# Letting V run four blocks ahead at the start of the last pass, preparing the tail, and holding three stores back

## The chip, the cores and the metric

The kernel runs on one core of one Trainium2 chip. The time is device microseconds of one execution. A profile shows one execution, and single executions of these kernels differ by several microseconds, so times are judged from the timed runs and the profiles are read for where the time goes.

## The reference, cut to what matters

Two layers, each grouped-query attention of one token over a cache of 65,536 positions (32 query heads on 4 K/V heads, head size 128), and a feed-forward block with squared ReLU, then the gradient of everything. Both layers share K, V and the weights.

```python
def _A_ref(x, k_cache, v_cache, wq, wo):        # cut
    q = (x @ wq) ...
    p = softmax(q k^T * Dh**-0.5); o = p v
    return o @ wo
x = x + A(layernorm(x)); x = x + B(layernorm(x))   # twice, same weights
_out, _vjp = jax.vjp(_f, A_x, A_k_cache, A_v_cache, A_wq, A_wo, B_w1, B_b1, B_w2, B_b2)
return (_out, *_vjp(grad_out))
```

The gradients of K and V are as large as the caches: 128 MB of stores, nearly all in the last pass.

## The kernel before: what the change and the argument touch

The kernel makes four passes over K and V. The last one, `attn_bwd4`, walks 4 groups of 16 blocks (a block is 32 x 128 positions of V or K, 1 MB) in steps of 8 columns, 256 items in all. Per block it turns V (`vT`), forms dP and X (`vS`), makes dV (`dV8`), and with K adds to dq and makes dK (`k8`). Each result block is stored.

```python
pipeline(items, [(vT, 0), (vS, TLEAD), (dV8, DV_LAG), (k8, B4_LAG)], bg, end)

def outer16(name, out, key, xt, gg, j1):          # dV and dK, cut
    if j1 == 0:
        state[key] = Slot(name, True)             # a result takes a slot ...
    ...
        evac(stg[:, jj:jj + 8, :]..., pg[:, :], kind="f32")
    if j1 + 16 == J:
        nc.gpsimd.dma_start(out=out, in_=stg)
        state.pop(key).free(stored=True)          # ... and gives it back once stored
```

Loaded blocks and finished results share one arena of 20 slots of 1 MB. Eight of these hold E (what earlier passes left for both layers) when the last pass begins; two come free at the end of each group, so blocks and results have 12 slots in the first group and 18 in the last. Loads are issued by SP, stores by GpSimd (POOL in the profile). Which free slot a load of the last pass takes is this rule (`AHEAD` is 9 steps):

```python
if load and PS["pass4"]:
    early = [i for t, i in by_age if t <= NOW["step"] - AHEAD]
    i = early[-1] if early else by_age[0][1]
```

At the end, after the last K matmuls give dq, the gradient of wq for the last group is made from rows of dq and of the layer input by eight rank-2 products (`g_outer`), stored as two pieces of 1 MB.

## Time and profile before

| what | before |
|---|---|
| time, median of the first 3 runs | 2013.33 us (2010.8 to 2014.11) |
| profiled span | 2015.4 us |
| busy share PE / DVE / ACT | 80 / 58 / 52% |
| bytes moved, mean rate | 794.97 MB, 394 GB/s |
| last pass | from about 1205 us on |

How to read it: at the full rate of about 420 GB/s the transfers fill most of the span, so only stretches with a lower rate can be won. In the last pass these are the opening and the end. The lines are in the prediction.

### The profile page before, as it was taken

To read this page: it belongs to the slowest core of one execution; us is meant where nothing else is said; L and a number is where in the kernel's file an instruction comes from. 1 tells how busy PE (TensorE), PEld (TensorE's weight loads), DVE (VectorE), ACT (ScalarE), POOL (GpSimd) and SP (SyncE) were. 2 spreads that over 40 slices of the span, in tenths; PEclk is the share of its full clock that TensorE was granted. 3 is DMA by queue.
4 is the path that set the end of the run, shared out by engine and by line. 5 is a ranking of instruction groups with operands and counts; after the bars stand their busy time and mean duration, and the time that the engine had idled before them with its cause. 6 is when DMAs were issued, how large, how long until landed. Compare 5 with 4: busy or idle time off the path is not lost. (4 is left out here: it accounts for less than half of the span.)

```text
span 2015.4 us, 67001 instructions
## 1 busy us (share of the span) xinstructions
PE 1613.8 (80%) x30210; PEld 1315.4 (65%) x30210; DVE 1175.3 (58%) x2358; ACT 1043.6 (52%) x1613; POOL 144.4 (7%) x332
## 2 busy tenths in 40 slices
PE   6877787687887787868787888788778988698896
PEld 6877777677777686767777785455445555455554
DVE  5655455255555544535454476586658777577675
ACT  3444344253443353426354365586657677577675
POOL 0000000000000000000000001121111111121111
PEclk9999899699899997999888998799879889798888
DMA  9999999999999998999999986999999999999995
GB/s 389 420 419 420 419 422 399 391 406 419 420 417 419 420 404 316 371 420 420 418 413 417 394 305 254 363 404 424 421 405 404 408 419 399 358 405 424 416 377 236
DMA packets 110845, 794.97 MB, mean 394 GB/s; under 512 B 9424, under 2 KB 9438, under 8 KB 49374
## 3 DMA queue, kind: packets, MB, share of 16 engines
q1 hardware_dynamic: 86510, 624.99, 76.3%
q0 software_dynamic: 24048, 165.70, 19.9%
q8 instruction: 236, 3.87, 0.8%
q14 instruction: 51, 0.42, 0.1%
HBM read 624.96 MB, written 165.69 MB: 392 GB/s over the span
## 5 line engine op out<-in xcount | busy, mean ns | idle before, releaser
L153 DVE COPY kt<-ps_tr 128x1024 bf16<-128x1024 bf16 x724 | 497.7, 689 | 481.3 <-PE ps_tr L936 255.4
L150 ACT CAST arena<-ps_gg 128x1024 bf16<-128x1024 f32 x452 | 440.0, 1010 | 226.0 <-PE ps_gg L1303 169.7
L936 PE MATMUL ps_tr<-ident_b,arena 128*128 128x128 bf16 x3840 | 311.3, 226 | 55.7 <-DMA arena<-in_A_k_cache_dram 41.4
L936 PEld LDWEIGHTS <-arena 128*128 128x128 bf16 x3840 | 235.2, 101 | 62.3 <-DMA arena<-in_A_k_cache_dram 44.4
L153 DVE CAST arena<-ps_gg 128x1024 bf16<-128x1024 f32 (+1 forms) x191 | 228.9, 1199 | 77.3 <-PE ps_gg L1303 43.6
L150 ACT COPY kt<-ps_tr 128x1024 bf16<-128x1024 bf16 x164 | 172.3, 1055 | 185.9 <-PE ps_tr L1128 125.7
L1303 PE MATMUL ps_gg<-GG,xt 64*128 64x512 bf16 x1024 | 214.1, 417 | 46.3 <-DVE arena L153 26.1
L1038 PE MATMUL ps_acc<-arena 128*128 128x64 bf16 (+4 forms) x4096 | 204.7, 195 | 49.4 <-DMA arena<-in_A_v_cache_dram 28.9
L1249 PE MATMUL ps_tr<-ident_b,arena 128*128 128x128 bf16 x1824 | 178.2, 236 | 39.7 <-DMA arena<-in_A_v_cache_dram 38.8
L954 PE MATMUL ps_sc<-L_qpad,kt 128*128 128x64 bf16 (+7 forms) x3584 | 183.9, 194 | 19.6 <-issue 12.3
L1019 ACT ACTIVATE arena<-S_sb,L_negm 128x128 bf16<-128x128 f32 x256 | 165.7, 1003 | 58.2 <-DVE L_negm L1004 58.2
L1128 PE MATMUL ps_tr<-ident_b,arena 128*128 128x128 bf16 x1920 | 155.8, 227 | 46.5 <-DMA arena<-in_A_v_cache_dram 45.2
L1038 PEld LDWEIGHTS <-arena 128*128 128x128 bf16 x4096 | 158.5, 100 | 52.6 <-DMA arena<-in_A_v_cache_dram 32.9
L1249 PEld LDWEIGHTS <-arena 128*128 128x128 bf16 x1824 | 121.1, 105 | 94.3 <-issue 51.0
L954 PEld LDWEIGHTS <-kt 128*128 128x128 bf16 x3584 | 153.7, 100 | 25.7 <-issue 15.3
L1128 PEld LDWEIGHTS <-arena 128*128 128x128 bf16 x1920 | 118.1, 102 | 50.0 <-DMA arena<-in_A_v_cache_dram 47.9
L1329 PE MATMUL ps_acc<-X,arena 128*128 128x64 bf16 (+3 forms) x2048 | 120.7, 199 | 23.0 <-DMA arena<-in_A_k_cache_dram 23.0
L1019 ACT ACTIVATION_READ_ACCUMULATOR arena<-S_sb,L_negm 128x1 f32 x256 | 128.0, 500 | 0.0
L1329 PEld LDWEIGHTS <-arena 128*128 128x128 bf16 x2048 | 87.8, 102 | 59.4 <-issue 34.2
L1303 PEld LDWEIGHTS <-xt 64*128 64x128 bf16 x1024 | 61.2, 94 | 86.7 <-issue 48.0
L1282 PE MATMUL ps_sc<-DOB,kt 128*128 128x64 bf16 (+3 forms) x1824 | 117.7, 200 | 0.0
L1173 PE MATMUL ps_acc<-dsT,arena 128*128 128x64 bf16 (+7 forms) x2048 | 104.0, 195 | 16.7 <-DMA arena<-in_A_k_cache_dram 12.2
(269 smaller groups left out, 2129.1 us busy)
## 6 DMA issues: line engine op xcount, KB each, us to landing
arena<-in_A_k_cache_dram SPq DMA_DIRECT2D x86, 2048.0 KB, 21.4
arena<-in_A_v_cache_dram SPq DMA_DIRECT2D x83, 2048.0 KB, 21.7
out_dram<-arena POOLq DMA_DIRECT2D x151, 1024.0 KB, 11.4
arena<-in_A_v_cache_dram SPq DMA_DIRECT2D x76, 1024.0 KB, 16.2
arena<-in_A_k_cache_dram SPq DMA_DIRECT2D x76, 1024.0 KB, 14.6
arena<-in_B_w_dram SPq DMA_DIRECT2D x32, 896.0 KB, 5.9
arena<-in_A_wq_dram SPq DMA_DIRECT2D x22, 1024.0 KB, 14.3
arena<-in_A_wo_dram SPq DMA_DIRECT2D x18, 1024.0 KB, 18.5
```

What stands on the lines that cost most here:

```text
L150: nc.scalar.copy(out=out, in_=in_)
L153: nc.vector.tensor_copy(out=out, in_=in_)
L936: nc.tensor.transpose(pt[:, i, :], kb8[:, i, :], ident_b[:, :])
L954: nc.tensor.matmul(state["ps_s"][:, s:s + w, :].rearrange("p a b -> p (a b)"), lhsT=kt[:, i, :], rhs=L["qpad"][:, g, 0:w, :].rearrange("p ...
L1019: nc.scalar.activation(out=E(p, g, c0, SU)[:, :, h], in_=S[:, h, :], func=ACTF.Exp, bias=L["negm"][:, g, su, h:h + 1], scale=SCALE, accum_ ...
L1038: nc.tensor.matmul(ps_o[:, 0:w, :], lhsT=vb8[:, i, :], rhs=E(p, g, c, w), start=(c % SU == 0), stop=(c % SU == SU - 1), skip_group_check=True)
L1128: nc.tensor.transpose(pt[:, i, :], vb8[:, i, :], ident_b[:, :])
L1173: nc.tensor.matmul(ps_dq[:, 0:w, :].rearrange("p a b -> p (a b)"), lhsT=kb8[:, i, :], rhs=dsT[:, s:s + w, :].rearrange("p a b -> p (a b)") ...
L1249: nc.tensor.transpose(pt[:, i, :], vb8[:, i, :], ident_b[:, :])
L1282: nc.tensor.matmul(state["ps_dp"][:, s:s + w, :].rearrange("p a b -> p (a b)"), lhsT=vt[:, i, :], rhs=DOB[:, g, 0:w, :].rearrange("p a b - ...
L1303: nc.tensor.matmul(pg[:, 512 * h:512 * h + 512], lhsT=xt[64 * h:64 * h + 64, j1 // 8 + m, :], rhs=gg[64 * h:64 * h + 64, :, :].rearrange(" ...
L1329: nc.tensor.matmul(ps_dq[:, 0:w, :].rearrange("p a b -> p (a b)"), lhsT=kb8[:, i, :], rhs=X[:, s:s + w, :].rearrange("p a b -> p (a b)"), ...
```

## The change

The intent: several V blocks are already in the arena when the last pass starts, so begin with V work alone, free slots sooner, and let loads go earlier. Let stores of the last group wait so that loads go first. Do before dq arrives whatever of the tail does not need dq. The diff, cut to its core:

```diff
+    V_LEAD = 4 * J // 8                                   # 16 items
+    V_SHIFT = lambda k: min(V_LEAD, max(0, (k - V_LEAD) // 3))
-    B4_LAG = TLEAD + J // 8 + 1
+    DK_LAG = TLEAD + J // 8 + 1
+    B4_LAG = DK_LAG + J // 8                              # K four items later
-        if load and PS["pass4"]:
+        if load and PS["pass4"] and not NOW["burst"]:     # first group: oldest free slot
...
+                if g == items[0][0]:                      # X of the first group in one slot
+                        state["Xs"] = Slot("xs", True)
...
+        def held(g, c8):                                  # 1, 2, 3 stores held in the last group
+            i = place[(g, c8)] - (len(items) - n_g)
+            return min(sum(8 * i >= k * n_g for k in (3, 4, 5)), state.get("cap", 3))
...
-                nc.gpsimd.dma_start(out=out, in_=stg)
-                state.pop(key).free(stored=True)
+                pend.append((out, stg, state.pop(key)))
+                while len(pend) > held(g, c8):
+                    store(state["evac"])
...
-        pipeline(items, [(vT, 0), (vS, TLEAD), (dV8, DV_LAG), (k8, B4_LAG)], bg, end)
+        NOW["burst"] = True
+        pipeline(items, [(vT, ~0), (vS, ~TLEAD), (eIn, 0), (eT, TLEAD), (dV8, DV_LAG), (xT, DK_LAG - 1), (dK8, DK_LAG), (k8, B4_LAG)], bg,
+                 list(end) + [(3 + 2 * n, cap(n)) for n in range(3)], lead=V_SHIFT)
...
+    def g_outer_last(pool, out_dram, a_cols, b_cols, c0): # input rows and slots first, 512 KB stores
...
-    ... [(12 + B4_LAG, last_v), (12, pre_load("wq4", ...)), (5, fill4)])
-    bg.drain()
-    run(gwq(lastg[3]))
+    ... [(12 + B4_LAG, last_v), (20, pre_load("wq4", ...)), (10, fill4)])
```

Stages marked `~` run up to 16 items ahead of the others. The lead melts by one item in every three. A few buffers are made smaller to pay for it.

More of the change, by code (lines that the diff above doesn't have):

```diff
@@ L149, in evac @@
             load["act"] += 0.17 + n * 0.00083
-            nc.scalar.copy(out=out, in_=in_)
-        else:
-            load["dve"] += cd
-            nc.vector.tensor_copy(out=out, in_=in_)
+            return nc.scalar.copy(out=out, in_=in_)
+        load["dve"] += cd
+        return nc.vector.tensor_copy(out=out, in_=in_)
     def col_from_dram(v1d, n, name):
@@ L167, in col_from_dram_f @@
         nj = n // P
-        rows = tmp.tile([nj // 4, 4 * P], BF, name="rows_f", tag="rows_f", bufs=1)
-        nc.sync.dma_start(out=rows[:], in_=v1d.rearrange("(s x) -> s x", x=4 * P))
+        sl = Slot("rows_f")
+        rows = sl.t[0:nj // 4, 0:4 * P]
+        nc.sync.dma_start(out=rows, in_=v1d.rearrange("(s x) -> s x", x=4 * P))
         pt = ps_mv([P, 4, 8], BF)
@@ L174, in col_from_dram_f @@
             nc.vector.tensor_copy(out=col[:, :, j], in_=pt[:, j, 0:nj // 4])
+        sl.free()
         return col[:, :, :].rearrange("p s j -> p (s j)")
@@ L178, in col_to_dram_f @@
         nj = n // P
-        rows = tmp.tile([nj // 4, P, 4], BF, name="rows_f", tag="rows_f", bufs=1)
+        sl = Slot("rows_f", True)
+        rows = sl.t[0:nj // 4, 0:4 * P].rearrange("s (p j) -> s p j", j=4)
         c3 = col[:, :].rearrange("p (s j) -> p s j", j=4)
@@ L184, in col_to_dram_f @@
             nc.vector.tensor_copy(out=rows[:, :, j], in_=pt[:])
-        nc.gpsimd.dma_start(out=v1d.rearrange("(s x) -> s x", x=4 * P), in_=rows[:].rearrange("s p j -> s (p j)"))
+        nc.gpsimd.dma_start(out=v1d.rearrange("(s x) -> s x", x=4 * P), in_=sl.t[0:nj // 4, 0:4 * P])
+        sl.free(stored=True)
     def col_to_dram(col, n, v1d):
@@ L247 @@
     HELD, BUSY = set(), set()
-    NOW = {"step": 0, "pairs": True, "wide": False}
+    NOW = {"step": 0, "pairs": True, "wide": False, "burst": False}
     def wide(i):
@@ L363, in touch_order @@
         seen, out = set(), []
-        maxlag = max(l for _, l in stages)
-        for i in range(len(items) + maxlag):
-            for t, lag in stages:
-                if 0 <= i - lag < len(items):
-                    g, c8 = items[i - lag]
-                    key = (t, g, c8 // J)
+        at = sorted((k + (lag(k) if callable(lag) else lag), n, k) for n, (t, lag) in enumerate(stages) for k in range(len(items)))
+        if True:
+            if True:
+                for _, n, k in at:
+                    g, c8 = items[k]
+                    key = (stages[n][0], g, c8 // J)
                     if key not in seen:
@@ L376 @@
     B3_LAG = TLEAD + HB // 8 + 3
-    B4_LAG = TLEAD + J // 8 + 1
+    DK_LAG = TLEAD + J // 8 + 1
+    B4_LAG = DK_LAG + J // 8
     DV_LAG = TLEAD + 1
+    V_LEAD = 4 * J // 8
     ITEMS = [order_by_unit(False, SU), order_by_unit(True, SU), order_by_unit(False, HB), order_by_unit(True, J)]
+    V_SHIFT = lambda k: min(V_LEAD, max(0, (k - V_LEAD) // 3))
     TOUCH = [touch_order(ITEMS[0], [("k", 0), ("v", FWD_LAG)]), touch_order(ITEMS[1], [("k", 0), ("v", FWD_LAG)]),
-             touch_order(ITEMS[2], [("v", 0), ("k", B3_LAG)]), touch_order(ITEMS[3], [("v", 0), ("k", B4_LAG)])]
+             touch_order(ITEMS[2], [("v", 0), ("k", B3_LAG)]), touch_order(ITEMS[3], [("v", V_SHIFT), ("k", B4_LAG + V_LEAD)])]
     def plan_keep(p):
@@ L793, in tasks, with pipeline, due @@
             fn()
-    def pipeline(items, stages, bg, end=(), holds=()):
-        maxlag = max(l for _, l in stages)
+    def pipeline(items, stages, bg, end=(), holds=(), lead=None):
+        def due(lag):
+            at = {}
+            for k, it in enumerate(items):
+                at.setdefault(k + lag + LEAD if lead is None or lag >= 0 else k + ~lag + lead(k), []).append(it)
+            return at
+        LEAD = 0 if lead is None else lead(len(items))
+        when = [due(l) for _, l in stages]
+        maxlag = max(l for _, l in stages) + LEAD
         for i in range(len(items) + maxlag):
@@ L804, in pipeline @@
             for n, (fn, lag) in enumerate(stages):
-                if 0 <= i - lag < len(items):
-                    fn(*items[i - lag])
+                for it in when[n].get(i, ()):
+                    fn(*it)
                 if n == 0:
                     tasks(i)
-            bg.step(i)
+            bg.step(max(0, i - LEAD))
             NOW["wide"] = False
@@ L995, in low @@
                 nc.vector.tensor_reduce(out=gm[:], in_=v["ptm"][:], axis=AX.X, op=ALU.min)
-                v["gmb"] = tmp.tile([R, P], F32, name="gmb")
+                v["gmb"] = tmp.tile([R, P], F32, name="gmb", bufs=1)
                 nc.vector.tensor_scalar(out=v["gmb"][:], in0=ones_f[0:R, :], scalar1=gm[:, 0:1], scalar2=None, op0=ALU.mult)
@@ L1197, in attn_bwd4 @@
         CCf = vec.tile([P, G, 2, R2], F32, name="CCf")
-        F2 = vec.tile([P, G, NSU, R2], F32, name="F2")
-        for i, L in enumerate((La, Lb)):
-            nc.gpsimd.tensor_copy(out=F2[:, :, :, i * R:(i + 1) * R], in_=L["fw"][:, :, :, :])
         state = {}
@@ L1215, in g_setup @@
                 nc.vector.tensor_tensor(out=CCf[:, g, 1, i * R:(i + 1) * R], in0=L["dOT"][:, sl], in1=L["rZ"][:, sl], op=ALU.mult)
-            ndt = dspool.tile([64, J, R2], BF, name="ndt4", tag="ndt4", bufs=1)
+            ndt = dspool.tile([64, R2], BF, name="ndt4", tag="ndt4")
             for i, L in enumerate((La, Lb)):
-                nc.vector.tensor_copy(out=ndt[:, :, i * R:(i + 1) * R], in_=L["nd2"][:, sl].unsqueeze(1).to_broadcast([64, J, R]))
+                nc.vector.tensor_copy(out=ndt[:, i * R:(i + 1) * R], in_=L["nd2"][:, sl])
             state["ndt"] = ndt
@@ L1223, in su_setup @@
             cf = tmp.tile([P, 2, R2], F32, name="cf")
-            nc.vector.tensor_tensor(out=cf[:, :, :], in0=CCf[:, g, :, :], in1=F2[:, g, su, :].unsqueeze(1).to_broadcast([P, 2, R2]),
-                                    op=ALU.mult)
+            for i, L in enumerate((La, Lb)):
+                sl = slice(i * R, (i + 1) * R)
+                nc.vector.tensor_tensor(out=cf[:, :, sl], in0=CCf[:, g, :, sl], in1=L["fw"][:, g, su, :].unsqueeze(1).to_broadcast([P, 2, R]),
+                                        op=ALU.mult)
             GG = []
@@ L1253, in vT, with eIn @@
                 state[("vt", g, c8)] = vt
+        def eIn(g, c8):
             if c8 % J == 0:
@@ L1256, in vT @@
                 nc.gpsimd.tensor_copy(out=split2(xin[:, :, :]), in_=E2(g, c8, J))
-                state[("xin", g, c8 // J)] = xin
+                state["xin"] = xin
         def x_transpose(src):
@@ L1269, in vS @@
                 g_setup(g)
-            if c8 == sufirst[(g, c8 // SU)]:
-                su_setup(g, c8 // SU)
-            if c8 % J == 0:
-                state[("xe", g, c8 // J)] = x_transpose(state.pop(("xin", g, c8 // J)))
             vt = state.pop(("vt", g, c8))
@@ L1279, in vS @@
                     nc.tensor.matmul(state["ps_dp"][:, :, :].rearrange("p c r -> p (c r)"), lhsT=sel2[:, :],
-                                     rhs=state["ndt"][:, :, :].rearrange("o c r -> o (c r)"), start=True, stop=False)
+                                     rhs=state["ndt"][:, :].unsqueeze(1).to_broadcast([64, J, R2]), start=True, stop=False)
                 w = min(4, J - s)
@@ L1288, in vS, with eT, xT, store @@
                 ps_dp = state["ps_dp"]
-                X = dspool.tile([P, J, R2], BF, name="X", tag="X")
+                if g == items[0][0]:
+                    if c8 == J - 8 + items[0][1]:
+                        state["Xs"] = Slot("xs", True)
+                    X = state["Xs"].t.rearrange("p (n j r) -> p n j r", j=J, r=R2)[:, c0 // J % 8, :, :]
+                else:
+                    X = dspool.tile([P, J, R2], BF, name="X", tag="X", bufs=3)
                 nc.vector.tensor_tensor(out=split2(X[:, :, :]), in0=split2(ps_dp[:, :, :]), in1=E2(g, c0, J), op=ALU.mult)
                 add_load(dve=0.13 + J * R2 * 0.00105)
-                state[("xd", g, c0 // J)] = (X, x_transpose(X[:, :, :]))
-                E_done(g, c0, J)
-        def outer16(name, out, key, xt, gg, j1):
+                state[("X", g, c0 // J)] = X
+        def eT(g, c8):
+            if c8 == sufirst[(g, c8 // SU)]:
+                su_setup(g, c8 // SU)
+            if c8 % J == 0:
+                state[("xe", g, c8 // J)] = x_transpose(state["xin"])
+        def xT(g, c8):
+            if c8 % J == J // 2:
+                state[("xt", g, c8 // J)] = x_transpose(state[("X", g, c8 // J)])
+                E_done(g, c8 - J // 2, J)
+        place = {k: i for i, k in enumerate(items)}
+        n_g = len(items) // G
+        pend = deque()
+        def store(ins):
+            out, stg, sl = pend.popleft()
+            st = nc.gpsimd.dma_start(out=out, in_=stg)
+            tc.add_manual_dep(st.ins, ins.ins.name, mybir.DependencyInfo(mybir.DependencyClass.Sync, mybir.DependencyReason.DATA),
+                              reason="stores follow the loads of later blocks")
+            sl.free(stored=True)
+        def held(g, c8):
+            i = place[(g, c8)] - (len(items) - n_g)
+            return min(sum(8 * i >= k * n_g for k in (3, 4, 5)), state.get("cap", 3))
+        def cap(n):
+            def f():
+                state["cap"] = n
+                while len(pend) > n:
+                    store(state["evac"])
+            return f
+        def outer16(name, g, c8, out, key, xt, gg, j1):
             if j1 == 0:
@@ L1306, in outer16 @@
                 jj = j1 + 8 * m
-                evac(stg[:, jj:jj + 8, :].rearrange("p j d -> p (j d)"), pg[:, :], kind="f32")
+                state["evac"] = evac(stg[:, jj:jj + 8, :].rearrange("p j d -> p (j d)"), pg[:, :], kind="f32")
             if j1 + 16 == J:
-                nc.gpsimd.dma_start(out=out, in_=stg)
-                state.pop(key).free(stored=True)
+                pend.append((out, stg, state.pop(key)))
+                while len(pend) > held(g, c8):
+                    store(state["evac"])
         def dV8(g, c8):
@@ L1314, in dV8, with dK8 @@
             if 2 * j0 < J:
-                outer16("gstv", half(GVv, g, b), "stv", state[("xe", g, b)], state[("GG", g, c8 // SU)][1], 2 * j0)
+                outer16("gstv", g, c8, half(GVv, g, b), "stv", state[("xe", g, b)], state[("GG", g, c8 // SU)][1], 2 * j0)
+        def dK8(g, c8):
+            b, j0 = divmod(c8, J)
+            if 2 * j0 >= J:
+                outer16("gstk", g, c8, half(GKv, g, b), "stk", state[("xt", g, b)], state[("GG", g, c8 // SU)][0], 2 * j0 - J)
         def k8(g, c8):
@@ L1320, in k8 @@
             su = c8 // SU
-            X, xt = state[("xd", g, b)]
+            X = state[("X", g, b)]
             if c8 == sufirst[(g, su)]:
@@ L1332, in k8 @@
             kv_done("k", g, c8)
+            if (g, c8) == items[len(items) // G - 1]:
+                state["Xs"].free()
+                NOW["burst"] = False
             if c8 == sulast[(g, su)]:
@@ L1336, in k8 @@
                     on_group(g)
-            if 2 * j0 >= J:
-                outer16("gstk", half(GKv, g, b), "stk", xt, state[("GG", g, su)][0], 2 * j0 - J)
         start_pass(p)
-        pipeline(items, [(vT, 0), (vS, TLEAD), (dV8, DV_LAG), (k8, B4_LAG)], bg, end)
+        NOW["burst"] = True
+        pipeline(items, [(vT, ~0), (vS, ~TLEAD), (eIn, 0), (eT, TLEAD), (dV8, DV_LAG), (xT, DK_LAG - 1), (dK8, DK_LAG), (k8, B4_LAG)], bg,
+                 list(end) + [(3 + 2 * n, cap(n)) for n in range(3)], lead=V_SHIFT)
     def rows2(cols, halves, rows, f=False):
@@ L1369, in rank2 @@
         evac(out, pg[:, 0:n], kind="f32")
+    def g_outer_last(pool, out_dram, a_cols, b_cols, c0):
+        ras = []
+        for a0 in (0, 4):
+            ra = pool.tile([66, 4 * P], BF, name="rowa", tag="rowa", bufs=2)
+            rows2(a_cols, (a0, a0), ra)
+            ras.append(ra)
+        sls = [Slot("og", True) for _ in ras]
+        yield
+        rb = pool.tile([66, 4 * P], BF, name="rowb", tag="rowb")
+        rows2(b_cols, (0, 4), rb)
+        yield
+        for a, (ra, sl) in enumerate(zip(ras, sls)):
+            og = sl.t[:, :].rearrange("p (j n) -> p j n", j=4)
+            rows = out_dram[a * 512:(a + 1) * 512, c0:c0 + 1024].rearrange("(p j) n -> p j n", j=4)
+            for j in range(4):
+                rank2(og[:, j, :], lambda r: f_cols(ra[r, :], j), lambda r: rb[r, :])
+                if j % 2:
+                    nc.gpsimd.dma_start(out=rows[:, j - 1:j + 1, :], in_=og[:, j - 1:j + 1, :])
+                yield
+            sl.free(stored=True)
     def g_outer(pool, out_dram, nA, nB, a_cols, b_cols, c0=0, a_f=False):
@@ L1625, in on4 @@
         else:
+            next(PRE["gwq"])
             PRE["rows"].run()
+            next(PRE["gwq"])
             dxn1 = ln_bwd(dn1[:], L1["n"], L1["rstd"])
@@ L1630, in on4 @@
             col_to_dram(dx0, D, out_1.rearrange("a b d -> (a b d)"))
+            run(PRE["gwq"])
     def last_v():
@@ L1640, in fill4 @@
         PRE["rows"].fill()
-    attn_bwd4(3, L1, L3, on4, bg, b4, [(12 + B4_LAG, last_v), (12, pre_load("wq4", lambda: wq_slabs(lastg[3], 2))), (5, fill4)])
-    bg.drain()
-    run(gwq(lastg[3]))
+        bg.drain()
+        PRE["gwq"] = g_outer_last(bgpool, out_4, [L3["n"], L1["n"]], [L3["dqT"][:, gsl(lastg[3])], L1["dqT"][:, gsl(lastg[3])]],
+                                  lastg[3] * 1024)
+        next(PRE["gwq"])
+    attn_bwd4(3, L1, L3, on4, bg, b4, [(12 + B4_LAG, last_v), (20, pre_load("wq4", lambda: wq_slabs(lastg[3], 2))), (10, fill4)])
     b4.close()
```

## The prediction

> **What bounds the kernel now.** I read the page's slices first, to see where the DMA engines are not full, then the windows of the last pass, then the waits of the queue that issues loads (SP), then the timeline at the opening, and last the chain of waits at the end.
>
> ```profile
> span 2015.4 us, 67001 instructions
> ...
> DMA  9999999999999998999999986999999999999995
> GB/s 389 420 419 420 419 422 399 391 406 419 420 417 419 420 404 316 371 420 420 418 413 417 394 305 254 363 404 424 421 405 404 408 419 399 358 405 424 416 377 236
> ```
>
> A slice is 50.4 us. Most of the span moves about 420 GB/s with the DMA engines full: the kernel is bound by transfers, except in a few places. Those that this change can reach are slices 23 to 25 (254 to 363 GB/s, the start of the last pass) and the last two (377, 236). The windows view cuts the last pass into opening, middle, last items and end; its columns after the window and its length are busy time of PE, PEld, DVE, ACT, POOL, then granted clock, DMA share and GB/s:
>
> ```profile
> 1215.00:1330.00 115.00, 90.58 (x1092) 55.04 (x1091) 74.14 (x129) 69.00 (x81) 20.38 (x40) 0.81 0.85 320
> 1330.00:1940.00 610.00, 507.26 (x6444) 320.42 (x6444) 435.48 (x755) 414.07 (x493) 107.19 (x198) 0.88 1.00 408
> 1940.00:1990.00 50.00, 48.63 (x622) 31.26 (x623) 37.70 (x63) 36.04 (x40) 8.95 (x15) 0.92 0.89 346
> 1990.00:2015.00 25.00, 10.57 (x111) 4.61 (x108) 10.29 (x27) 8.15 (x10) 2.51 (x4) 0.62 0.32 127
> ```
>
> Against the middle's 408 GB/s the opening leaves (408 - 320) x 115 us = 10.1 MB unmoved, 24.8 us; items and end together leave 62 x 50 + 281 x 25 = 10.1 MB, again 24.8 us. The middle, against 422 GB/s, loses 610 x 14 / 422 = 20 us. So about 70 us of the last pass's 800 us are not transfer at the full rate, and no version of this pass can win more.
>
> Why the opening is slow: the SP queue, the timeline of SP, and PE's wait.
>
> ```profile
> SPq L331 <- PE ps_sc L1282: 34.9, 3, 24.3
> ...
> 1202.93 0.34 SPq L331 DMA_DIRECT2D arena<-in_A_k_cache_dram  x1
> ...
> 1206.56 0.34 SPq L331 DMA_DIRECT2D arena<-in_A_k_cache_dram  x1
> ...
> 1231.20 4.79 SPq L331 DMA_DIRECT2D arena<-in_A_k_cache_dram  x2
> ...
> 1246.43 1.03 PE L1329 MATMUL ps_acc<-X,arena 128*128 128x64 bf16 x16 [7.19 <-DMA arena<-in_A_k_cache_dram]
> ```
>
> Two K blocks of 1 MB go out at 1203 and 1207; the third waits 24 us, because the slot given to it still held a V block and then a block of results to store. The first stores are only issued from 1224 on, so between 1218 and 1226 almost nothing moves. Then PE, which runs in order, stands 7.2 us until that third K block is there, and everything behind it (dV, dK, their stores) stands too.
>
> At the end, the chain of waits after the last K matmuls, when no load is left:
>
> ```profile
> 1990.93 0.37 PE ps_gg L1303
> 1991.30 2.10 PE ps_acc L669 x64
> ...
> 1993.76 1.23 DVE arena L153
> ...
> 1995.15 0.70 DVE rowb L153
> ...
> 1996.91 0.70 DVE rowa L153
> ...
> 2001.73 0.58 ACT rowa L150
> ...
> 2002.36 1.23 PE ps_gg L1368 x2
> 2003.61 1.24 DVE arena L153
> 2004.89 1.05 PE ps_gg L1368 x4
> 2005.96 1.24 DVE arena L153
> 2007.23 0.49 issue
> 2007.73 0.75 POOLq L1671
> ```
>
> From dq complete (1990.8) to the end is 24.6 us: rows of dq and of the layer input, eight rank-2 products, two stores of 1 MB, the second issued at 2007.73 and landed at 2015.4 (7.7 us).
>
> **What the Trainium skill says.** "DMA: Bandwidth & Descriptors", section "Issuing engines are not separate DMA queues": loads from SP and stores from GpSimd run on the same 16 engines and interleave. The trace agrees: the middle shows a share of 1.00 with both kinds in flight, so a store held back gives its time to loads. The same page, "Anatomy of one DMA", gives about 2 us fixed plus bytes / 436 GB/s, 4.4 us for 1 MB; the last store took 7.7 us with its issue, so I use the trace. "TensorE: Matmul & The Clock Gate", section "HAM oscillation", says a PE idle gap over about 3.4 us brings the slow clock back. The trace agrees: the granted clock was 0.50 in 1242 to 1250, just after the 7.2 us wait. "Perfetto Trace Analysis", section "Optimization Strategy", says a kernel with several regimes may gain from interleaving them; the change does that at both ends.
>
> **The change part by part.** No matmul, no evacuation and no byte is removed (the instruction count on PE is the same, 60186); the change only moves work. The first three passes keep their order.
>
> 1. Opening. Seven V blocks are already in the buffer, transposed, when the pass starts. Now dP and X of the first four are made at once, and dV, dK and K follow 16 items later, with V's lead melting over the first group. By the program's order the slots free at the start now go to K, K, V and K loads (before: two K, the others to results), so four loads leave at about 1203 to 1209, not two. K's matmuls come four items after dK's (before: in the same step), X waiting in a ring. So the third K block is there when it is wanted: the wait of 7.2 us goes. With it goes part of the slow clock: PE was busy 32.0 of 40 us in 1250 to 1290 at a clock of 0.72; at the middle's 0.88 the same work is 32.0 x (1 - 0.72 / 0.88) = 5.8 us less, of which I count 4, as evacuations limit too. A further 2 MB early fills idle DMA time: 2 / 0.408 = 5 us. Against: 32 matmuls of a V block took 1.67 us, and three blocks now precede the first dV store, some 5 us later to the store path. Sum: -7 - 4 - 5 + 5 = -11 us, of the 24.8 lost.
>
> 2. One slot of 20 is taken for the X ring for the first group: fewer slots for loads and stores in 200 us. Estimate +1.
>
> 3. Middle. dK no longer waits for K's landing: PE's waits on K blocks in the middle are 12.3 us (K matmuls waiting for K loads). But DMA is full there, so a wait removed mostly becomes another. I give -2 us.
>
> 4. Tail prepared. The input rows (two of them: eight r_cc casts, sixteen small matmuls, evacuation, 1.3 to 2 us each on the chain) are made ten steps before the end; only the rows of dq remain after dq. Before, first product at 1997.65, last evacuation ends 2007.2. After: dq, cast and row matmuls 1.5 us, row evacuation 0.7, then eight products of about 1.0 us each (two PSUM buffers, evacuations 1.01 on ACT and 1.24 on DVE side by side), with the 2.1 us of the dn matmuls between: 1990.8 + 2.2 + 2.1 + 8 = 2003, 4 us sooner. Stores are halves of 512 KB: 7.7 - 0.5 / 0.408 = 6.4 us for the last, instead of 7.7. Sum: -5.5, and some slack in the order of PE: -7.
>
> 5. Three stores held in the last group. 3 MB of store move behind the loads: at 408 GB/s up to 7.5 us earlier loads. But in 1940 to 1990 PE is busy 48.6 of 50 us and DVE and ACT 75%: the last items are bound by compute, so earlier loads mean little. I give -3, and +1 for K's four later items at the end. The held stores are let go over the last steps, before the final products, so they should not queue in front of the last store.
>
> Total: -11 + 1 - 2 - 7 - 2 = -21; with a little for the middle's one long stall (a 17.5 us DVE wait around 1710 to 1727 for a weight slab, which a new order may hide) I say -23: 2013 - 23 = 1990 us.
>
> **Rivals.**
> - The wait only changes its place: the fifth and later loads still need slots that hold results, whose stores now start later. For: in the middle SP's waits are nearly all for stores (462 us in 82 waits), so slots, not matmuls, gate loads. Then the opening gives 3 us and the total is -10: about 2003.
> - The transfers catch up fully: with V ahead, stores run at the evacuation rate from the start, the opening loses only the 8 us before its first store, the middle's waits on V and K shrink, the held stores work in full. Opening -17, middle -8, tail -15: -40, 1973. For: PE, DVE and ACT are at 83, 71 and 68% in the middle. Against: evacuations and loads share one ring of slots.
> - The tail backs up: held stores (3 MB, 7.5 us) run into the final stores and eat step 4's gain. Against: DMA share was 0.32 in the last 25 us. Then -14: 1999.
> - A burst of matmuls lowers the granted clock later; the clock is 0.88 in the middle, and this would cost 5 to 10 us.
>
> **Range and chances.** Runs of the kernel before spread by 0.15%, so the range is that of the steps: opening -3 to -17, tail -5 to -15, middle +5 to -8. I take 1975 to 2004. Faster by 2% needs 1973, nearly the second rival in full: 0.12. Slower by 2% would need 40 us of new waiting with the same work: 0.01.
>
> **What would show it.** Right: four loads before 1210 on SP, PE's 7 us wait on K gone, more than 345 GB/s in the pass's first 115 us; the last product within 13 us of dq, end within 19 us of it. Wrong: the fifth load waiting until 1240 or later with DMA idle before it; a PE wait on the new V loads; a last store that lands over 8 us after its issue; the middle under 400 GB/s because of the lost slot.

## More of the kernel before

One more line of the windows is needed later. Its columns are, after the window and its length, the busy time of PE, PEld, DVE, ACT and POOL, then the granted clock, the DMA share and GB/s:

```profile
1330.00:1400.00 70.00, 58.44 (x764) 36.28 (x764) 51.62 (x98) 50.32 (x58) 12.57 (x23) 0.95 1.01 423
```

Directly after its slow opening the kernel before runs with full DMA engines.

## The result, and the profile after

The changed kernel took 2022.55 us (median of 4 runs, 2019.69 to 2026.81) beside 2012.07 us for the kernel before (4 runs, 2010.41 to 2014.11). The ratio is 1.0053, with a 95% interval of 1.0028 to 1.0078. A ratio here is the mean time of one kernel's runs over that of the other's of the same rounds, so not quite the ratio of the medians quoted. The change is within 2%, and slower. The prediction was 1990 us with a range to 2004, so the time missed the range on the far side of "no gain".

The slices of the changed kernel's page (50.4 us each):

```profile
GB/s 390 420 419 420 419 421 402 392 400 419 419 418 422 421 398 312 373 420 420 419 417 413 392 327 246 366 360 375 419 415 423 417 413 395 401 416 426 365 344 304
```

And its windows of the last pass:

```profile
1215.00:1330.00 115.00, 93.04 (x1152) 57.46 (x1146) 71.20 (x125) 64.84 (x73) 18.84 (x36) 0.82 0.80 308
1330.00:1400.00 70.00, 51.52 (x641) 32.18 (x640) 43.69 (x82) 41.56 (x52) 10.08 (x20) 0.83 0.96 368
1330.00:1940.00 610.00, 502.52 (x6348) 315.02 (x6346) 429.10 (x762) 412.42 (x493) 105.36 (x196) 0.87 0.99 401
...
1990.00:2018.00 28.00, 13.05 (x146) 6.70 (x143) 10.28 (x23) 9.35 (x11) 6.03 (x10) 0.64 0.66 263
```

The opening did not get faster (308 after 320 GB/s). The stretch behind it, full before, fell from 423 to 368. The middle fell from 408 to 401. The last 28 us move 263 GB/s where the last 25 of the kernel before moved 127: more was left to store. Of the signs that the prediction named for being wrong, two are there: a fifth load after 1240 us with the DMA engines idle before it, and PE waiting for the new V loads. The last store is issued at 2009.3 us and has landed at 2014.8 us, 5.4 us later, so the sign "over 8 us after its issue" is not there.

Landings here are the times at which a DMA's completion is counted in the trace, on the clock of the other views. The span runs on for 3.1 to 3.2 us after the last landing in all 17 traces: the program closes with drains and barriers, and nothing is moved. The kernel before shows it, first with the issue and landing of its last store (size, then us to landing; this view counts 4.6, the completions 4.5), then with its last 3.1 us:

```profile
out_dram<-arena POOLq DMA_DIRECT2D x1, 1024.0 KB, 4.6
...
2012.30:2015.40 3.10, 0.00 (x0) 0.00 (x0) 0.00 (x0) 0.00 (x0) 0.00 (x0) 0.50 0.00 0
```

**The opening.** SP's timeline, the longest of SP's waits from 1200 to 1340 us (us in total, times, longest), the first store on POOL, and PE's waits on loads from 1203 to 1330 us:

```profile
1201.73 3.71 SPq L334 DMA_DIRECT2D arena<-in_A_k_cache_dram  x2
1205.49 0.42 SPq L334 DMA_DIRECT2D arena<-in_A_v_cache_dram  x1
1212.00 0.33 SPq L334 DMA_DIRECT2D arena<-in_A_k_cache_dram  x1
1241.84 0.33 SPq L334 DMA_DIRECT2D arena<-in_A_v_cache_dram  x1
```

```profile
SPq L334 <- DMA out_dram<-arena: 93.5, 12, 29.4
```

```profile
1231.94 0.58 POOL L1327 DMA_DIRECT2D out_dram<-arena  x1 [5.59 <-PE ps_gg L1426]
```

```profile
PE ps_acc L1384 <- DMA arena<-in_A_k_cache_dram: 10.2, 2, 5.6
PE ps_tr L1262 <- DMA arena<-in_A_v_cache_dram: 8.2, 2, 4.9
```

The first store of the kernel before and PE's waits on loads, for comparison:

```profile
1224.04 0.58 POOL L1309 DMA_DIRECT2D out_dram<-arena  x1 [1.86 <-ACT arena L150]
...
PE ps_acc L1329 <- DMA arena<-in_A_k_cache_dram: 10.7, 2, 7.2
PE ps_tr L1249 <- DMA arena<-in_A_v_cache_dram: 7.0, 1, 7.0
```

Four loads do leave by 1212 us, and the old wait of 7.2 us on K is gone. But the first store comes 7.9 us later, the fifth load waits up to 29.4 us for a slot whose result must first be stored, and PE meets other waits. Together its waits on K and V loads are 18.4 us here and 17.7 in the kernel before: the wait of 7.2 us was traded for others.

**The lead and what becomes of it.** X of the ninth block and of the first block of the second group, in the kernel before and then in the changed one (where X of the first group lies in an arena slot):

```profile
1310.67 0.68 DVE L1290 TENSOR_TENSOR X<-ps_sc,arena 128x512 bf16<-128x512 f32 x1
...
1407.74 0.68 DVE L1290 TENSOR_TENSOR X<-ps_sc,arena 128x512 bf16<-128x512 f32 x1
```

```profile
1269.92 0.68 DVE L1306 TENSOR_TENSOR arena<-ps_sc,arena 128x512 bf16<-128x512 f32 x1
...
1408.87 0.68 DVE L1306 TENSOR_TENSOR X<-ps_sc,arena 128x512 bf16<-128x512 f32 x1
```

V's side is 40.8 us ahead at the ninth block, and 1.1 us behind at the seventeenth. All of the lead is spent within the first group, and nothing of it is left as time. While it melts, SP and PE of the changed kernel wait as follows from 1330 to 1400 us (SP's longer waits for stores are left out):

```profile
SPq L334 <- PE ps_tr L1262: 12.2, 2, 10.2
```

```profile
PE ps_tr L1262 <- DMA arena<-in_A_v_cache_dram: 17.0, 4, 6.7
```

In the kernel before PE's waits on V in these 70 us were:

```profile
PE ps_tr L1249 <- DMA arena<-in_A_v_cache_dram: 6.4, 2, 4.2
```

PE, which is ahead with V, now waits 17.0 us for V loads. Two K loads, with V loads behind them on SP's queue, wait 12.2 us for slots that PE's V transposes have not released, a wait that the kernel before does not have in this stretch. So the two may wait for each other at times, though no view shows one such circle whole. The DMA share is 0.96 at 368 GB/s.

**The last group.** The windows line of 1850 to 1940 us, where stores are held, of the kernel before and the changed one:

```profile
1850.00:1940.00 90.00, 77.58 (x963) 47.87 (x962) 63.65 (x111) 58.62 (x65) 17.30 (x31) 0.87 1.01 416
```

```profile
1850.00:1940.00 90.00, 74.50 (x974) 46.10 (x971) 61.60 (x114) 57.98 (x67) 16.03 (x27) 0.89 0.91 364
```

The held stores do not make room that loads fill: the share falls to 0.91. At the end, POOL's stores of the changed kernel:

```profile
1996.15 1.58 POOL L1327 DMA_DIRECT2D out_dram<-arena  x3 [2.53 <-DVE arena L152]
2006.65 0.53 POOL L196 DMA_DIRECT2D out_dram<-rows_c  x1 [8.92 <-DVE rows_c L195]
2007.18 2.87 POOL L1447 DMA_DIRECT2D out_dram<-arena  x4
```

Three stores of 1 MB go out together at 1996.15. Then POOL has nothing to do for 8.92 us before a store of 2 KB (the gradient of x) whose rows are not ready, and the four halves of the last weight gradient, the first of them evacuated at about 2002, all leave behind it. The Trainium skill says why this can be: "DMA: Bandwidth & Descriptors", section "Anatomy of one DMA", states that any semaphore wait happens on the issuing sequencer before dispatch. The trace agrees, with these 8.92 us.

### The profile page after: what moved, and what is told of

Its sections match the earlier page's. It is cut to its first block, busy times and chain, and to the rows that moved or that the text cites. A ratio compares the mean times of both kernels' runs of the same rounds, so it can differ in the third digit from the quotient of the medians.

```text
span 2018.0 us, 66993 instructions
## 1 busy us (share of the span) xinstructions
PE 1616.7 (80%) x30210; PEld 1319.7 (65%) x30210; DVE 1168.4 (58%) x2376; ACT 1043.3 (52%) x1611; POOL 144.2 (7%) x332
## 5 line engine op out<-in xcount | busy, mean ns | idle before, releaser
L150 ACT CAST arena<-ps_gg 128x1024 bf16<-128x1024 f32 (+1 forms) x453 | 441.3, 1011 | 244.9 <-PE ps_gg L1352 186.0
L950 PE MATMUL ps_tr<-ident_b,arena 128*128 128x128 bf16 x3840 | 309.8, 226 | 57.9 <-DMA arena<-in_A_k_cache_dram 39.7
L1262 PE MATMUL ps_tr<-ident_b,arena 128*128 128x128 bf16 x1824 | 181.9, 235 | 66.1 <-DMA arena<-in_A_v_cache_dram 64.2
L1142 PE MATMUL ps_tr<-ident_b,arena 128*128 128x128 bf16 x1920 | 161.3, 232 | 41.4 <-DMA arena<-in_A_v_cache_dram 40.8
L1052 PEld LDWEIGHTS <-arena 128*128 128x128 bf16 x4096 | 159.8, 100 | 51.0 <-DMA arena<-in_A_v_cache_dram 33.5
L968 PEld LDWEIGHTS <-kt 128*128 128x128 bf16 x3584 | 153.0, 100 | 24.6 <-issue 17.8
L1293 PEld LDWEIGHTS <-kt 128*128 128x128 bf16 x1824 | 84.5, 103 | 45.6 <-issue 44.4
L1384 PE MATMUL ps_acc<-X,arena 128*128 128x64 bf16 (+3 forms) x1536 | 92.6, 198 | 25.1 <-DMA arena<-in_A_k_cache_dram 24.8
```

Of the source, the lines that this page charges most:

```text
L150: return nc.scalar.copy(out=out, in_=in_)
L950: nc.tensor.transpose(pt[:, i, :], kb8[:, i, :], ident_b[:, :])
L968: nc.tensor.matmul(state["ps_s"][:, s:s + w, :].rearrange("p a b -> p (a b)"), lhsT=kt[:, i, :], rhs=L["qpad"][:, g, 0:w, :].rearrange("p ...
L1052: nc.tensor.matmul(ps_o[:, 0:w, :], lhsT=vb8[:, i, :], rhs=E(p, g, c, w), start=(c % SU == 0), stop=(c % SU == SU - 1), skip_group_check=True)
L1142: nc.tensor.transpose(pt[:, i, :], vb8[:, i, :], ident_b[:, :])
L1262: nc.tensor.transpose(pt[:, i, :], vb8[:, i, :], ident_b[:, :])
```

## The experiments

Theory after this reading: the time is lost in three places, namely the hold (stores crowd the end), the lead (with its slot, or with the rule that loads take the oldest slot), and POOL's queue. The prepared tail should be a gain that these hide. Rivals: K's delay is the cost; or none is, and the order as such costs.

### Round 1: parts of the change taken out

**No lead** (`a_nolead`). The X slot and the oldest-slot rule go with it.

```diff
-    V_LEAD = 4 * J // 8
+    V_LEAD = 0
-                if g == items[0][0]:
+                if False:
-        NOW["burst"] = True
+        NOW["burst"] = False                              # cut: the X slot's release goes too
```

> The changed kernel with the V lead and its X ring slot taken out (lead 0, X in three ordinary buffers), the rest kept. Theory A (the lead costs: the first store goes out 8 us later, 1231.9 against 1224.0, the fifth load waits 29 us for a store, and 5 MB less have moved by 1500 us): faster than the changed kernel by 5 to 12 us, ratio to before 0.995 to 1.001, first store near 1224. Theory B (the loss sits in the tail: held stores and the order of the store queue): no gain, ratio 1.004 to 1.007.

Measured: 2023.24 us, ratio to the kernel before 1.0051 (1.0029 to 1.0073), as slow as with the lead. The opening was not what made the change slow as long as stores are held.

**No hold** (`a_nohold`).

```diff
-            return min(sum(8 * i >= k * n_g for k in (3, 4, 5)), state.get("cap", 3))
+            return 0
```

> The changed kernel with no store held in the last group. Theory B (holding only moves stores into a tail that is bound by compute, so dq comes no sooner and the stores crowd the end): 2 to 6 us faster than the changed kernel, ratio 1.000 to 1.004. Theory A: within 2 us of the changed kernel. If holding works as meant (loads earlier), it is 3 to 7 us slower, ratio 1.007 to 1.009.

Measured: 2018.95 us, 1.0030 (1.0009 to 1.0051). It points to the hold, though the two intervals overlap, so this alone did not settle it.

**The 2 KB store on another queue** (`a_spout`).

```diff
-            col_to_dram(dx0, D, out_1.rearrange("a b d -> (a b d)"))
+            col_to_dram(dx0, D, out_1.rearrange("a b d -> (a b d)"), nc.sync)
```

> The changed kernel with the 2 KB store of dx issued from SP instead of GpSimd, so the four last halves of the weight gradient do not stand behind it (they stood 8.9 us in the changed kernel, issued 2007.2 to 2009.4 though the first half was evacuated at 2001.9). If that order costs the tail: the last store is issued right after the last evacuation and the end comes 2 to 4 us sooner, ratio 1.003 to 1.004. If the tail is set by the last evacuation alone: within 1 us.

Measured: 2024.7 us, 1.0056 (1.0033 to 1.0079). The 8.92 us wait of POOL was gone from the trace, and the time did not move. The most striking line of the changed kernel's tail was not a cost: the held 3 MB fill the DMA engines meanwhile (a share of 0.93 from 1997 to 2007 us, and the last of the three lands at 2008.7). In `a_spout` the first half leaves at 2004.5 us, with the held stores still under way until 2009.9, and lands 6.7 us later; in `a_nohold` the first half took 3.1 us.

**The split stages and the prepared tail alone** (`a_tailonly`): no lead, no hold, and K not delayed (`B4_LAG = DK_LAG`).

> The changed kernel without the lead, without held stores and with K in the same step as dK again: what is left is the prepared tail and X turned two items later. Prediction's step 4 alone (a tail 7 us shorter): ratio 0.9965. If the tail's gain is eaten by the order of the store queue: 0.999 to 1.001. If the split of dK from X costs time by itself: above 1.002.

Measured: 2014.41 us, 1.0012 (0.9987 to 1.0036). Most of the loss is gone, and there is still no gain, although in the trace only 19.5 us pass from dq to the end (24.8 before).

### Round 2: single parts, and the suspicion of K's delay

**The prepared tail put into the kernel before** (`b_prep`).

```diff
-    ... (12, pre_load("wq4", ...)), (5, fill4)])
-    bg.drain()
-    run(gwq(lastg[3]))
+    ... (20, pre_load("wq4", ...)), (10, fill4)])     # and g_outer_last, as in the change
```

> The kernel before with the prepared tail alone (input rows, slots and background work done ten steps before the end, stores in halves). In the runs so far dq to the end took 24.8 us before, 19.5 to 20.2 us with the prepared tail where no store was held. Theory C (the prepared tail is worth 5 us, the other parts lose it again): ratio 0.996 to 0.999. Rival: draining the background ten steps early pushes its work onto the last items, dq comes later by as much: 1.000 to 1.002.

Measured: 2012.05 us over 22 runs, 1.0000 (0.9991 to 1.0009). This is one of the two tightest numbers: the prepared tail is worth nothing, to within 0.09%. Its trace shows where the saving goes. PE's last pieces and POOL's last store of this kernel:

```profile
1997.83 0.62 PE L1368 MATMUL ps_gg<-rowb,rowa 2*128 2x512 bf16 x2 [0.83 <-DVE arena L153]
...
1999.77 0.61 PE L1303 MATMUL ps_gg<-GG,xt 64*128 64x512 bf16 x2 [0.77 <-DVE arena L153]
```

```profile
2002.28 0.56 POOL L1309 DMA_DIRECT2D out_dram<-arena  x1 [1.30 <-issue]
```

The rank-2 products (L1368) are done first, and the last dK block (L1303) now comes behind them. Its 1 MB store, issued at 2002.28, is the last to land, at 2006.4, and the span ends at 2009.6. From the landing of the last K or V load to the end, 47.9 us pass here and 48.6 in the kernel before; from dq to the end it is 24.2 and 24.8. The work was put in another order, not taken away.

**K not delayed**, with the hold (`a_klag0`) and without it (`a_nohold_klag0`).

```diff
-    B4_LAG = DK_LAG + J // 8
+    B4_LAG = DK_LAG
```

> The changed kernel with K's matmuls back in the step of dK (lead and held stores stay). Theory D (the four-item delay puts all dK evacuations between the last X and dq: 13.2 to 14.6 us where K is delayed, 10.4 us before, 3.7 us with K undelayed and no lead): dq 3 to 5 us earlier than the changed kernel, ratio 1.002 to 1.004. Rival (K's delay is harmless, the loss is in the middle): ratio 1.005 to 1.007.

> The changed kernel with neither held stores nor delayed K: lead and prepared tail alone. If the two parts undone cost about 4 us each and add up: ratio 0.999 to 1.002, as for the kernel without lead, hold and delay (1.0012). If the lead costs by itself: above 1.003. If the lead gains as predicted (11 us): below 0.997.

Measured: 2024.51 us, 1.0063 (1.0048 to 1.0078), and 2018.14 us, 1.0037 (1.0024 to 1.0050). Taking the delay out did not help in either. The theory that K's delay costs fell. The pair is a second measurement of the hold: 1.0063 against 1.0037.

**One slot less in the kernel before**, for the first group of the last pass (`b_slot`).

```diff
+        state["idle"] = Slot("idle", True)                # before the pass
...
+            if (g, c8) == items[len(items) // G - 1]:
+                state["idle"].free()
```

> The kernel before with one of its 20 slots taken out of use during the first group of the last pass, as the X ring does. If a slot is worth what the changed kernel lost between 1320 and 1500 us (5 MB, 12 us): ratio 1.003 to 1.006. If slots are not what limits there: 0.999 to 1.002.

Measured: 2016.18 us, 1.0021 (1.0008 to 1.0035), some 4 us for one of the 12 slots that blocks and results have then, over a quarter of the pass. I had counted 1.

### Round 3: what in the lead costs (all with nothing held)

**No lead** (`n_nolead`) and **the slot rule of the kernel before** (`n_noburst`, `NOW["burst"] = False`).

> The changed kernel without held stores (1.0030 before's time) and now without the lead too: delayed K and prepared tail are left. Theory E (the lead's opening gain is given back while it melts: 348 to 370 GB/s in 1330 to 1400 us with the lead, 402 to 423 without; net cost 4 to 6 us): ratio 0.999 to 1.0015, and 400 GB/s or more in 1330 to 1400. Rival (the lead nets nothing, K's delay and the split cost the rest): 1.0025 to 1.004.

> The changed kernel without held stores, the lead kept, but loads of the first group choose their slot by the old rule (freed nine steps ago or more, the youngest of them) and not simply the oldest free one. Theory F (the oldest-slot rule makes the loss of 1330 to 1400): that stretch at 400 GB/s or more, ratio 0.998 to 1.001. Rival (the lead itself or the lost slot): stretch still below 380, ratio 1.002 to 1.004.

Measured: 2015.45 us, 1.0013 (1.0004 to 1.0022), and 2013.28 us, 1.0009 (0.9996 to 1.0022). Both are nearer to the kernel before than `a_nohold` at 1.0030. I then took the oldest-slot rule for a cost of 0.2%.

**Shorter leads with X in pool buffers, no slot taken** (`n_lead2_pool`, `n_lead1_pool`). A lead of four with eight or seven such buffers could not be built: the pool wanted 17.2 or 16.2 KB a partition, and 14.7 were left.

```diff
-    V_LEAD = 4 * J // 8
+    V_LEAD = 2 * J // 8          # the other: J // 8
-                    X = dspool.tile([P, J, R2], BF, name="X", tag="X", bufs=3)
+                    X = dspool.tile([P, J, R2], BF, name="X", tag="X", bufs=5)   # the other: 4
```

> The changed kernel without held stores, with a lead of two V blocks (8 items) whose X lie in five ordinary buffers, so that no slot is lost. Theory G (the lost slot, worth 0.2% by itself, is what makes the lead lose): ratio 0.998 to 1.001 and 1330 to 1400 near 410 GB/s. Rival E (the melting lead itself): half the loss stays, 1.001 to 1.003, the stretch at 370 to 400.

> The same with a lead of one V block and four ordinary buffers. First store near 1226. Theory E: nearly as without a lead, ratio 0.999 to 1.002. If a short lead is the good dose of the idea (K loads early, stores not late): below 0.998.

Measured: 2025.75 us, 1.0065 (1.0052 to 1.0077), and 2011.84 us, 0.9996 (0.9988 to 1.0004). Giving the slot back did not make a lead of two good, so the slot alone is not the cost of the lead. A lead of one neither gains nor loses.

### Round 4: do the costs add?

**The whole change with the old slot rule** (`a_noburst`), and the old rule with leads of two and one (`n_lead2_pool_nb`, `n_lead1_pool_nb`). Each edit is `NOW["burst"] = False`.

> The changed kernel with all of its parts (hold too), but loads of the first group keep the rule of the kernel before for their slots (the youngest of those freed nine steps ago) instead of taking the oldest. Theory: the hold (+0.25%) and the slot rule (+0.2%) are separate costs that add: 1.0053 - 0.0021 = 1.003, about 2018.5 us. Rival: the rule only costs where nothing is held, because the stretch of 1330 to 1400 us stayed slow without it (363 GB/s against 348): then 1.005, 2022 us.

> Lead of two blocks, X in five pool buffers, no slot taken, nothing held, and the kernel before's slot rule. With the oldest-slot rule this kernel ran at 1.0065, worse than a lead of four (1.0030) and of one (0.9996), which no theory of mine explains. Theory: the rule lets a load wait for a store at particular leads; without it 1.001 or less, below 2014 us. Rival: a lead of two blocks is slow by itself (the order of K and V loads that it makes): 1.005 or more, over 2022 us.

> The best version so far (lead of one block, X in four pool buffers, nothing held; 0.9996 with the oldest-slot rule), with the kernel before's slot rule. If the rule costs 0.2% at every lead: 0.9975, about 2007 us, which would beat both kernels by a little. If the rule only matters when V runs far ahead: 0.9996, the same as before.

Measured: 2026.69 us, 1.0066 (1.0045 to 1.0087); 2020.6 us, 1.0045 (1.0031 to 1.0060); 2014.93 us, 1.0011 (0.9998 to 1.0023). My theory of the slot rule fell. Going back to the old rule changed the four pairs by -0.21% (nothing held), +0.13% (held), -0.20% (lead of two) and +0.15% (lead of one), which is no effect on the mean. Why a lead of two is the worst stays open: its two traces read 72.4 and 72.6 MB from 1200 to 1600 us, all others 73.2 to 75.5, but they do not show why.

### The pairs together

Each part was taken out in several settings, so its effect can be averaged over pairs of ratios. The width is the root of the summed squares of the half-intervals, divided by the number of pairs, taking the intervals as independent.

| part | pairs, with minus without, in % | mean |
|---|---|---|
| hold | 0.23, 0.26, 0.38, 0.57 | +0.36 ± 0.13 |
| lead, with its slot and rule | 0.02, 0.17, 0.25 | +0.15 ± 0.16 |
| K's delay | -0.10, -0.07, 0.01 | -0.05 ± 0.15 |
| prepared tail | in the kernel before | 0.00 ± 0.09 |

The hold's pairs are the changed kernel and `a_nohold`, `a_klag0` and `a_nohold_klag0`, `a_nolead` and `n_nolead`, `a_noburst` and `n_noburst`. Hold and lead together are 0.51 of the 0.53% measured: 7.2 and 3.0 us of 10.7 (each per cent figure times 2012 us). Only the hold is told apart from zero. Three of its four pairs join ratios of different rounds; the one pair of the same rounds, `a_klag0` and `a_nohold_klag0`, gives 0.26 ± 0.20.

What the hold does in the traces, counted from the trace's records of single transfers (profile of one execution each; held / not held):

| pair | GB/s in 1850-1940 | MB read in 1850-1940 | last K or V load landed, us | MB written after it | us from it to the end |
|---|---|---|---|---|---|
| changed / `a_nohold` | 364 / 392 | 16.5 / 18.0 | 1976.8 / 1979.6 | 11.9 / 9.0 | 41.2 / 37.4 |
| `a_noburst` / `n_noburst` | 372 / 393 | 18.2 / 16.5 | 1986.0 / 1974.4 | 12.3 / 8.8 | 44.5 / 37.7 |
| `a_klag0` / `a_nohold_klag0` | 397 / 424 | 17.8 / 17.8 | 1969.5 / 1967.3 | 16.3 / 11.4 | 54.9 / 47.0 |
| `a_nolead` / `n_nolead` | 360 / 418 | 15.5 / 17.9 | 1974.4 / 1979.3 | 11.9 / 8.3 | 40.1 / 36.4 |

The rate falls in every pair, on the mean by 33.5 GB/s; over 90 us that is 3.0 MB, just what is held. The loads get none of it on the mean, though single pairs differ: they read 17.0 MB where 17.5 are read without the hold, and the last load lands no sooner (1976.7 against 1975.2). The reason can be read from SP: its waits for stores, for the loads that it issues from 1850 to 1960 us, are 100.2, 113.4, 107.1 and 101.6 us with the hold and 92.7, 101.8, 100.0 and 96.8 without, longer in all four pairs. The bytes are written after the last load instead, and the stretch from there to the end is 3.7 to 7.9 us longer in all four, 5.5 on the mean. Of these, 3.1 us on the mean lie between dq and the end (23.5 to 24.1 us with the hold, 19.9 to 21.3 without). POOL of `a_nohold` shows the same end without the crowd (its first and its last half):

```profile
2004.78 0.72 POOL L1447 DMA_DIRECT2D out_dram<-arena  x1 [5.33 <-DVE lnb_t L235]
...
2010.69 0.71 POOL L1447 DMA_DIRECT2D out_dram<-arena  x1 [0.99 <-ACT arena L150]
```

The last half, issued at 2010.69, lands 3.1 us later at 2013.8, and the span ends at 2017.0.

No version beat the kernel before. The best, `n_lead1_pool` and `b_prep`, tie with it.

## Why the prediction was wrong

**Step 1, the opening (-11).** What I said of single events came nearly true: four loads early (the fourth at 1212.0, not by 1210), the 7.2 us wait gone, the first store later (in the profiles of seven kernels with a lead of four it is issued at 1227.4 to 1234.0 us, in six without a lead at 1222.1 to 1224.9; 7.9 us between the two kernels, where I had said 5). The failed terms are "-7" for the wait and "-5" for "a further 2 MB early fills idle DMA time". By 1330 us the two kernels have moved nearly the same, 525.4 MB before and 525.2 after; by 1400 us the changed one is 4.1 MB behind (555.0 and 550.9). The wait on K was not worth its length because loads and stores, not PE, set the pace, and later waits replaced it: 18.4 us of PE's waits on loads against 17.7. I had also misread the wait. The third K load, at 1231.20, was let go by PE's matmuls of a V block, with no store in between; but PE's 7.2 us ended with the landing of the fourth, at 1246.39. That one was issued at 1235.66, just after a store had landed at 1235.59. So a store stood in the path of the very wait that I meant to remove. A block loaded early is one that is not loaded later: a lead gains only if transfers fill time in which nothing else would have moved, and the slots for that came no sooner than the stores did. My first rival named this mechanism, a fifth load that waits for stores. But it still gave the opening 3 us, and nothing in it said that the lead would be paid back in a stretch that had been full. With seven traces of a lead of four at 345 to 370 GB/s in 1330 to 1400, and 386 to 424 in the six without, that repayment is shown; its cost in time, 0.15 ± 0.16%, is not told apart from zero.

**The clock (-4, within step 1).** The granted clock of 1215 to 1330 us was 0.81 before and is 0.82 after: the wait of 7.2 us went, and the clock stayed. (The 0.50 that I read "just after" the wait began within it: the trace's clock records have it from 1241.6 to 1255.2 us, the wait ended at 1246.4.) In single executions the clock differs more than that. In 1218 to 1226 us the profile of the changed kernel had 0.50, and that of `a_nohold`, whose only edit concerns the last group, had 1.00. A term read from the clock of one execution was not safe.

**Step 2, the slot (+1).** Too small where it could be measured: +4 us in the kernel before. I had reckoned with one slot of 20, where E holds eight of them and the slot was one of 12.

**Step 3, the middle (-2).** The long stall that I hoped to hide is eased (the slice of 358 GB/s from 1714 us on now has 401), but the stretches of the melting lead and of the held stores lose more, and the middle went from 408 to 401 GB/s. Taking K's delay out of the changed kernel changed nothing, so it neither paid nor cost.

**Step 4, the prepared tail (-7).** The chain that I added up was right in the changed order (19.5 us from dq to the end in `a_tailonly`, against "within 19"; in the changed kernel itself it was 23.7 us), and its worth was zero. I took the work moved before dq as free, although the windows line that I printed had PE busy 48.6 of 50 us there, and I used this very line in step 5. In `b_prep` the last dK block and its store simply became the end. One reading in this step was wrong: the last store of the kernel before landed 4.5 us after its issue, not 7.7, for the last 3.1 us of the span move nothing. So there was no slow last store, and the 4.4 us that I took from "DMA: Bandwidth & Descriptors", section "Anatomy of one DMA", and put aside agree with the trace; for 512 KB the same fit gives 3.2 us, and the last half of `a_nohold` took 3.1.

**Step 5, the held stores (-3 + 1).** This is the largest error, by sign: +7. The failing sentence is "3 MB of store move behind the loads: at 408 GB/s up to 7.5 us earlier loads". Loads in this kernel wait for slots, and a held store keeps its slot (SP waited 7.8 us longer for stores on the mean of the four pairs); I had written in a rival that "slots, not matmuls, gate loads" and did not apply it here. And "they should not queue in front of the last store" did not hold: the three still occupy the DMA engines until 2008.7 us, and where the halves are free to leave sooner (`a_spout`) the first takes 6.7 us instead of 3.1. My third rival, the tail that backs up, had the mechanism. It only took away step 4's gain; in fact there was no gain to take, and the crowding was a net loss.

The common fault is the adding of gains: five steps, each read at its own wait, nearly all with the same sign, in a kernel whose DMA engines are full for most of the pass. The sums had slips too: the first rival's total should have been -13, not -10; the slow ends of the three ranges (-3, -5, +5) add up to -3, or 2010 us, where I took 2004; and the 60186 given for PE's instructions stands on no page, which count 30210 matmuls and 30210 weight loads in both kernels. The range (1975 to 2004) did not even hold "nothing gained", which `b_prep`, `a_tailonly` and `n_lead1_pool` all turned out to be.

## What to carry to other kernels

If loads and results share a ring of buffers and loads already wait for them, as here, a store held back does not hand its DMA time to loads, for it keeps the buffer that the next load needs; see who waits for what before moving stores. Work moved ahead of a critical result is free only if the engines there have room, so read the busy time of the stretch that it moves into. And a lead built from blocks that are already loaded must be paid back, so count the bytes moved by a later moment rather than the events at the start.

## What the Trainium skill lacked or had wrong

- I found no page that gives the time that a kernel's own closing drains and barriers take at the end of a profiled span. Here it is 3.1 to 3.2 us after the last landing in all 17 traces, 2.3 to 2.4 of them until POOL's drain ends. Taken for transfer time, it made a store of 4.5 us look like one of 7.7.
- "TensorE: Matmul & The Clock Gate", section "HAM oscillation", speaks of idle gaps over about 3.4 us. In the changed kernel's profile the clock fell to 0.50 in 1218 to 1226 us after PE had been busy 11.9 of the 15 us before, its longest wait in 1197 to 1218 shown in the timeline being 0.82 us; `a_nohold` was busy 12.3 of those 15 us and kept 1.00. The same page's "A second HAM failure mode" names short idles between groups of matmuls, which may fit; no run here tells.
- "Perfetto Trace Analysis", section "Optimization Strategy", says that interleaving regimes may help. It lacks the other side: where buffers are shared, holding stores for loads lowered the rate in four of four pairs (by 33.5 GB/s on the mean) and cost 0.36 ± 0.13%.
